# A different start and other load layouts for a linear-attention and ELU-MLP kernel on one core

## The chip, the cores and the metric

The kernel runs on one core of one Trainium2 chip. The metric is the device time of one execution in microseconds (us); lower is better. A core has a matrix engine (PE, whose weight loads are listed apart as PEld), a vector engine (DVE), a scalar engine (ACT) for exponentials and copies, GpSimd (POOL) and a sync engine (SP) that only issues transfers. Transfers (DMAs) are issued from queues of SP, ACT and POOL and carried by 16 DMA engines. POOL's own queue is the only one here that also changes the type (f32 to bf16) on the way.

## The reference

Inputs q, k, v are (8 batches, 8 heads, 576 positions, 64) in f32, w_phi is 64x128, w_in 512x2048, w_out 2048x512. The output is 4608x512 in f32.

```
def phi(x):
    proj = x @ w_phi
    proj = proj - max(abs(proj), axis=-1)
    return concatenate([exp(proj), exp(-proj)])
q_p, k_p = phi(q), phi(k)
kv  = sum over positions of k_p (outer) v
z   = sum over positions of k_p
out = (q_p @ kv) / (q_p . z + 1e-6)          # linear attention
x   = out, heads side by side: 4608 x 512
h   = x @ w_in
g   = h if h > 0 else exp(h) - 1             # ELU
return g @ w_out
```

## The kernel before, in words

**Attention.** The work is cut into 16 "quads": quad i is batch i//2 and four of its heads. In each head 512 positions are "main" and the last 64 are the "tail". For k and q, quad by quad: a transpose (kT, qT), a projection with w_phi (tile pk; for q also one with the operands exchanged, pq), the exponentials of plus and minus the projection on ACT (EK for keys at L697, Eq for queries at L851), and the row maximum of the magnitude on DVE (L659). The maxima of the keys give factors em on ACT (L726), and POOL multiplies v by them (vs at L748 for the main part, vst at L758 for the tail). PE then sums keys times values (pkv, L894), and queries times that (pn, L948 and L962). DVE combines the signs (tot, L997 and L1003), POOL divides (x, L1045 and L1074), and x is transposed (xT).

For the first five quads k and q are transposed on PE against an identity matrix (`ident`), L583 for the main part and L561 for the tails; later quads use transposing DMAs from SP. A tail transpose takes 64 positions of two heads, a 64x128 block. Tails of k and q of one batch share one staging tile t_b, k on partitions 0 to 63 and q on 64 to 127, loaded as 64 partitions of 8 heads with 64 numbers each.

**MLP.** Nine chunks of 512 tokens, one for each batch's main part and a ninth for all tails. mm1 (ph<-xT,w_in, L1241; for chunk 0 in halves of 256 tokens, L1256), exponential e on ACT (L1269), u = e − 1 on POOL (L1273), g = max(min(u, 0), h) on DVE (gT, L1285), mm2 (po<-w_out,gT, L1343), a copy out of PSUM to o_sb on ACT or DVE (L1369, three o_sb buffers), and a store (L1378, L1382). In mm1 the weights that are loaded into PE are 128 neighbouring columns of w_in, in mm2 they are 128 tokens of gT.

**What sets the order.** The order on each engine is written out while the program is built. A `Planner` (L125 to L315) is given every operation with an assumed cost per engine, what it depends on, and which of the eight PSUM banks it takes. It walks through assumed time and gives each engine that is free the ready operation of the lowest rank; where an operation may run on ACT or DVE, it chooses. The ranks are in the string RANKS, two characters for each operation in the order of their making. POOL may have up to eight loads outstanding. Before assumed time 60 the planner puts matrix products of zeros (`fill`, L1545) where it expects PE to idle, for half of the expected gap, and 32 of them stand at the start.

**The start.** SP's queue loads k half 0 of quad 0 (as f32, into buffers of v) and then w_phi twice (L1412, L1421), ACT's queue k half 1. ACT casts these to bf16 (L1443, L1454). POOL first builds the identity (L1427), and then issues casting loads, half of q, the k tails, half of k, k of batch 1, and then the rest of batches 0 and 1, w_in in two halves (L385) and w_out in four parts (L388), mixed by the planner with its arithmetic. w_in lies in one tile, with partition p holding row p of each block of 128; w_out likewise, so that each load of four blocks brings four separate rows of 512 numbers to each partition. Batches 2 and later are loaded when earlier quads have released the staging tiles (two buffers for each).

Of the kernel before, what the change touches and what calls it, by code (L numbers as in the profile page):

```python
# [34 lines left out]
    "00Fb02Fl011z8i04050309070B080A060D0F0H0K0C0M0J0G0d0e0ETUPETXPbE5OG2hOa9GN25g97E4"  # L35
    "Rt0W0TOm0R0SNX0b0QOC0P0OOk0Z0X0U0V320o0n0I0L0g0f6aLiLj0YKGKLKW6ZMdMf0N0cMM0a47Oc"
    "VTVQKKKFWECTOnAUNL45BmBiBs3C2F44BlBcBt3B2E432MB9Ba3637BY5T5V5F5O9i4L5qGp6DEI84IN"
    "E6Ml9HMs9FN38D8EKyWBVXK+MbMcMtMPMOKzMWWGNi2YMaWAMZ4M2t2Z2a2c3x3z38SnSlWCWHWDWF4B"
    "5859313A302-48MwWJVYWI4PWKAp2+Aa4g7F8M897I728J3E3S4Y3IFzFY9Y6+5S5v5J5KE33d3qEU6I"
    "5tAx6t2g6EDo4O6fCa2LFR9bC77R3XHu5w6T4q3rC95j6H6v5P7U6Y6eAJ5YH76w9w545p71AIAeCy6G"  # L40
    "4V9uAS3l7DBnAb3i4k7g7W5r9XLN7i5k7M5XDL7v7Z3L6N8B4f6p537z4d2b706L5sGTIk6l7o9rF69f"
    "AA6U85D1CmBH8oAdB0APD24l6O7p835yAE7G8N7x8O8g9T7r7w7s8w9pCx4R8FLa8e1V2zBS6W2U413-"
    "2O5D57BD4+50BE4v5ABF4y5I2N515B5G5H8P5d5f4n4o5m5l1wC0C18t8s8q8z1vCBCA9V9W8b8a567T"
    "3o3s8y9eA-65EA3M3W8h4h2P693O4m8l4i2R7YAH4x4T5R61628v8j91CFB3Kt8d1S2xCZ6X1W6x6y4Q"
    "CHCI4aCMCG4ZCQCO4XCPCdBA4p39CSCb3D6S66676F4j5N2w7L7K757476732X7a7b7Q7O7P7N6J7V3g"
    "3h775W3mAt2V5z8c685+8f6C6M4J5Q5x8Z6B5-6u40A8BhBg90A29DA99CCcGiCn929hAKFED0AQ7CEo"
    "9EA099EiTNFhEcGZW8JgDHILVrITB-FfUIIbE-FyVpW3FJI6BoW5BQHI8A869xEWAMDyCU2WAW6i2r6d"
    "AL6K9z2p9B987k796r9ZFc9cVqAX8HACGs3JFiFMGnI7Sp3KEpDuERF3ANC3BIDAGAGDFoE02v5M3u5U"
    "4C6hAzAw4rCjB2Ay4zCi3a7E818Y8U968R8S828T8X958Q8V64DnDm8WCDC8BwBuBxBvCgCf3N6c6bAD"
    "A5A4A63f8K8L8p8u8rCC2u6k7S78C655CoUOEFTPFdESTOF7EEW6GlGBV4HPGM4FGODVDK7B7ADS8x2e"  # L50
    "6P2j6V4D7JA79d9lAZ9gFrCRAB9+AR9m9n5nDDEG9v9tA39aGg9S9Q8IGd4WGyGvGXGUGVGQ4HCtCpEk"
    "EmEsEu8-BkC4C2Dx6zAOVBGI8n2k2q8m2Q2m603Z2s6q2i2oA+244sW1H3H4273FAFFZKXObEP8kAkSb"
    "He9-JDRhD9FIIyRIHpJQFmFpHcJSF9JAIDL2JF93I51oEHB1DlMI21LEIKA120LPIHFg88CeHGIMDbJb"
    "H08GCkBqJYEz9sKaDpEwECF5D7GjJlE8IOJhIwKx3+RBHkICGtIh9PTRGhHEEbD-BKDQDRD6DrDv5u4I"
    "4E7j6A7hCrDJAu4c7q7t7XWNWQWgWnWPWiWhWOWkWjWRWmWlFHWLWMWfWeW9WVWTWUWSWXWWAlWdWcCv"
    "ChCwCl5o4u4tWbWYWZWa7uFWCKCJDiAsENAmEVDW7eSgEQSi7d9jN87c8+QxQvDXTBT+RJF2FnUaUc87"
    "6-F1FX80AYBdAnBJBZAjAqBeAhAiBXAcAr9yBLBNBOBMIuEMELE1E2IrIsBVS6TyJMJRJPJLAgC+C-B6"
    "B7B8BBDYSsBzByJOHdTiD4SrIGBrB5IFB4LFDj9ULGDM949RIfATKZFDEqErR-RFDa6g4eHTF829DZHz"
    "DGIiHBISFBI4CqG8DkI8IjDPDB26JoBTHsFsEf8CI2LHIoFAGbHKJKExGoE7BCFjGmGkEKJwIaEDL0EJ"
    "GYBbI-G1GFBWFPKJGKAvK6GeFkG3FKFFIENeIQHWG+IRGHNRGuCYO8JBMxPOQaHmLOJfM1LbGRHjCsJ2"  # L60
    "KUBjD3BfV+DF3328DO6jCzBG9A1U1T9K1a1h9J1g1c9I1b1iQw1Q1R1Z1dG21p1m1l1n3435Dq1y1xId"
    "2I2J2KCW1+1-1r1q1u1sBUToJNL3IcF4G6D86RDCEj5iHnBP4-HoBR52DwHy9qDE635h7fI0H-O7ItB+"
    "C53bD+AGDN4w3w3p6s3t3k6m3n3j6o3y3vJH3P3T2C2B5Z5c7-5e5a7y7+D55C5E49424A46CV3Y3V4U"
    "4K4N4SEBKY3e3c3QIlEOIA3UFwG0KIH5HLH9FqEaJUFuEYEZH6GcHAGzEdEeJTJ7MjJEFLJ6InIzI9M8"
    "MkK5GwJXJ9KOGLHOLkKHH8FGK-HgIJHMKiJzIeF+LmGxU7HNN-DzDUIqL1NtEnOrLWIBFNLMGCKcEtN5"
    "MePyJnHFQyK4IpKjNUQuE9LINWS9JZO3MEMgPMP9QEK1O5Q-QmUo7HPaRQTJMBMUVsNIM9IvMJQ3ReK2"
    "1k221j234G6QGfDh3R4bFt1GE+1814Ev1617F0191DEy151A5L1H1I1C1BFCDfDeDcDgEgEhGaFUFV1M"
    "1L1N1OGGGPGS1X1f1Y1eGWI11F1E2yNHDsNGDtM5JWKpKVHQF-M4M7G4MFMAHHJ-K7HJO2JIJJKEJ+5b"
    "TaG9FQFxFvP0Q4QBP2QfQ6P7QCQ7P5QDQFMn9k9oQdQJGqOAOEOFODGrDdGJRKRMT2T5T3T7HiNPNQUU"
    "UDUSUBNYO1PnPpP1JcH+ImKAOTT1SzK0N4PsOSS+S-JyRYTMNvP+TQSj3G3HPYO4RbVJR9TFPz2HN1U3"  # L70
    "QH2TLBPKR02fNMPqQ+2lLtOwQpAVTAPCQRCERcPGQVRpHlOYQZPBSUOLQgM0QcRERyTdPiOPS5VWPPVa"
    "SxVMMiLAR1ViRgLXPZV8PXU9LzTgMXUNQbS3L+LeUiSALVO6LqLpCXR6LsL-LDLfTZTDM-MzRURSJpLl"
    "GE1JDI1KG5EXPmKmJkJ3HDMhKBHvHqJ5LKHrK9HxIxK8I+LLHUHSHRLSLQJeDTElG-FOKPJmJxNAN99N"
    "9M9L9OJiPuPt7lCN7m7nNTLJPRPQ1tNwTVIgTSIYVEUKIZVKUEIUVCUFIVVuUHIWVvURRfSBSCMVMHK3"
    "JCETPoIXJjPT0q0wPS0l0sPV0t0mPW0p0uJ413Kb0v0r110x0y0+0z0-10L8RzUQ0j0h0i0kKDVtVoRl"
    "RkRsRqL9Ri1P122GLgNBLhMuQUPNOZQ9OHPHQ8OBPFQYP6OdRdPIPLROPhPjJdNZLYUjUqVANaCuUWTp"
    "LwUMUTTfLoUYSMVmMDVfSVUCLcV3VGN6KeVgW7VRR+V-V9MoSZS0VDOMKhTYUePARXSwVZNSSaS4UZOW"
    "SuOgUwORRVRvVeS2SWR4RAMySYQMSPMqTCLuLvLxQGTHJqHCI3KrQjNxQoKQKRKqRTQSKoJtJuKkMmQ5"
    "G7J0J1BpQIOiHtJvKuOOLTONTnUnUmTmUbUhTtUpUfT-UvU+SXAoAfUyUsQQShSdRHRGSfQXL7UVUX2S"
    "2D2n2ALUVPVSFSFeFTFaPxPwCL2dU5KMVwKNVxM+NfNgRRNhTxKCV1U1KwV0TvKvU2TwNyVHVIM6LrR7"  # L80
    "LdKsNrLnJaVkHZHwVlU4HXVOHaHVVjHYHbVnRnRoVdVcU-SLSJV6SKV7V2KSNcNdVUVNVhVVLRUJUGUt"
    "TlUuTkQrRDTbTcU0L4T9KfRPSvVLMrKgOXNORWOVNKL5OUN+L6S1LZMvT8T6TITGJrQWUdPcJsUgSeLC"
    "KlTWMKRLJVU8UPPrJGQAGNQqKnVFQeSTNkMCR5OpM3KdRjSDNzOIP-OqNbSNKTQ2NDNVQLUzNqSGJ8Rr"
    "NsRaQOQzNETjQiMGMSQlOeTqNmSOR8QKM2NpNlOjNoO0OoMLPeOtSmQsMpP3O+MRVzNJOvPkOyUkOlPJ"
    "NnQhNuRCO-VbRZU6OxSqT4RuMQMYPUS7OsV5UrSoMNOKQtTuPdQPQ0TTPfTzTsNCNFR2QnTeO9MTT0Rm"
    "PgOQP8UxOzUASyPvOuTrLyQkP4OfSSRNPDUlSETEPlSRS8SQH2HfIIIPSHStN7NNOJOhULTLVyW0W2W4"
    "QTTKRwRxQ1ScSFSIQNSkN0Nj6nH1Th25HhR3"
# [231 lines left out]
def kernel(  # L319
# [11 lines left out]
    P = 128  # L331
# [46 lines left out]
    w_in_sb = consts.tile([P, N_CT, DFF], BF16)  # L378
    w_in_r = moe_w_in.rearrange("(ct p) j -> p ct j", p=P)
    w_out_sb = consts.tile([P, N_JT, DM], BF16)  # L380
    w_out_r = moe_w_out.rearrange("(jt p) o -> p jt o", p=P)

    def load_w_in(half):
        j = slice(half * (DFF // 2), (half + 1) * (DFF // 2))
        nc.gpsimd.dma_start(out=w_in_sb[:, :, j], in_=w_in_r[:, :, j])  # L385

    def load_w_out(jt):
        nc.gpsimd.dma_start(  # L388
            out=w_out_sb[:, jt:jt + 4, :], in_=w_out_r[:, jt:jt + 4, :]
        )  # L390
# [10 lines left out]
    def staged(b, n):  # L401
        if (b, n) not in kqv:
            kqv[b, n] = stage.tile(
                [P, H * D if n == 3 else BW],
                FP32 if n == 2 else BF16,
                name="kqvt"[n] + "_b",
            )
        return kqv[b, n]
# [9 lines left out]
    def load_tails(eng, n, b):  # L418
        if n < 2:
            eng.dma_start(  # L420
                out=staged(b, 3)[n * TAIL:(n + 1) * TAIL, :].rearrange(
                    "p (h d) -> p h d", d=D
                ),
                in_=(k, q)[n][b, :, MAIN:S, :].rearrange("h j d -> j h d"),
            )
            return
# [66 lines left out]
    def plan_quad(i):  # L493
# [33 lines left out]
        for n in range(2):  # L527
# [30 lines left out]
            def tail_transpose(e, n=n, t0=t0, tr_rows=tr_rows, trt=trt):  # L558
                t = psum(trt, [P, P], BF16, "trt")
                for s in range(2):  # L560
                    nc.tensor.transpose(  # L561
                        t[:, s * TAIL:(s + 1) * TAIL],
                        kqv[b, 3][tr_rows, t0 + s * P:t0 + (s + 1) * P],
                        ident[tr_rows, tr_rows],
                    )

            def tail_copy(e, n=n, trt=trt):
                f = nc.scalar.copy if e == "ACT" else nc.vector.tensor_copy
                f(in_tile(n)[:, 8, :], trt.tile)
# [7 lines left out]
            for j0, j1 in parts:  # L577
# [10 lines left out]
                def copy(e, tr=tr, j0=j0, j1=j1, n=n):  # L588
# [6 lines left out]
                    [main if len(parts) < 2 else landed[0, 0, 3 + j0 // 4], *prior],  # L595
# [14 lines left out]
            o2 = add({"PE": 0.06}, tail_transpose, [tail], new=[trt], key=key + 0.01)  # L610
# [158 lines left out]
        for c in range(3):  # L769
            for sg in range(2):  # L770
                vs_ops[c].append(
                    add(
                        {"POOL": 1.0 if c < 2 else 0.58},
# [14 lines left out]
        for c in range(3):  # L788
# [3 lines left out]
            def queries(e, c=c, pair=pair, pair_f=pair_f):  # L792
                blocks = slice(c, 8, 2) if halves else slice(4 * c, 4 * c + 4)
                project_halves(1, range(8)[blocks], pair)
                for par in range(2):
# [10 lines left out]
            def tail_queries(e, pair=pair, pair_f=pair_f):  # L806
# [11 lines left out]
            o = add(  # L818
                {"PE": 0.44 if c < 2 else 0.22},
                queries if c < 2 else tail_queries,  # L820
                [moved[1][0 if c < 2 else 1], *old("out")],
                new=pair + pair_f,
                mode=1 if c < 2 else 0,
                key=first + 0.4 + 0.2 * c,
            )
            ops["q"].append(o)
# [12 lines left out]
            for par, bank in enumerate(pair_f):  # L839
# [13 lines left out]
                for sg in range(2):  # L853
# [4 lines left out]
                            [o, landed["zero"]] if c == 2 else [o],  # L858
# [27 lines left out]
        for s in range(2):  # L886
# [24 lines left out]
            def kv_copy(e, s=s, bank=bank):  # L911
# [6 lines left out]
                {"PE": 0.65},  # L918
# [501 lines left out]
    for c in range(2):  # L1420
        nc.sync.dma_start(out=wst[c * D:(c + 1) * D, :], in_=w_phi)  # L1421
# [160 lines left out]
```

## Time and profile before

| | |
|---|---|
| median of 3 runs | 360.99 us (360.65 to 361.04) |
| the profiled execution | 361.48 us |
| its span, first to last instruction | 359.6 us |
| PE busy | 346.3 us (96%), of it fills from 0 to 50 us: 13.98 |
| DVE, ACT, POOL busy | 268.8, 256.5, 244.7 us |
| granted PE clock | 1.00 throughout |
| DMA | 86668 packets, 43.46 MB |
| first exponential of keys (EK, ACT) | starts at 7.36 us |
| first scaling of v (vs, POOL) | starts at 14.56 us |
| first product of mm1 / of mm2 | starts at 33.9 / 42.3 us |

Times inside a profile are counted from the start of the span. A busy PE is not PE at its peak, since the ends of pipelined products are modelled. A number in brackets behind an instruction is the idle time of its engine just before it, with what ended it.

### The profile page before, as it was taken

The numbers are of one execution on the slowest core, as the hardware profiler recorded it, in microseconds if no ns is written. First come the engines' busy times: TensorE is split into PE (matmuls) and PEld (weight loads), VectorE is DVE, ScalarE is ACT, GpSimd is POOL, SyncE is SP. The second block draws the span as 40 slices with busy tenths as digits, with TensorE's granted clock in tenths as the row PEclk, the third lists the DMA queues.
The fourth block names the chain that finished last, engine by engine and source line by source line (L and its number), as shares of the span: only waits on it lengthen the run. The fifth ranks groups of instructions, "written<-read, shape, count | busy, mean of one in ns | idle before, by whom it ended". The sixth has DMA issues, their size and how long they took to land.

```text
span 359.6 us, 8973 instructions
## 1 busy us (share of the span) xinstructions
PE 346.3 (96%) x3379; PEld 196.5 (55%) x3427; DVE 268.8 (75%) x580; ACT 256.5 (71%) x565; POOL 244.7 (68%) x342
## 2 busy tenths in 40 slices
PE   8888999999999999999999999999999999999995
PEld 7666776656554655455545555554456444444444
DVE  5989878989998899769977989999866812662600
ACT  5999977799779777985599888596994514553521
POOL 8699999298969797697677697366379622552500
PEclk9999999999999999999999999999999999999999
DMA  9999999999699799599759606682210331001013
GB/s 145 285 221 206 204 188 119 217 131 141 91 186 212 110 203 126 143 113 234 77 133 187 98 6 129 121 170 58 56 40 30 66 91 60 0 29 41 20 58 89
DMA packets 86668, 43.46 MB, mean 121 GB/s; under 512 B 55648, under 2 KB 80608, under 8 KB 86624
## 3 DMA queue, kind: packets, MB, share of 16 engines
q1 hardware_dynamic: 57632, 26.62, 36.5%
q0 software_dynamic: 28320, 15.47, 33.2%
q10 hardware_dynamic: 672, 0.79, 0.8%
q8 instruction: 27, 0.44, 0.5%
q14 instruction: 17, 0.14, 0.1%
HBM read 36.77 MB, written 9.44 MB: 128 GB/s over the span
## 4 chain that ended last, share of the span: by engine, by line
PE 78%; POOL 7%; ACT 4%; DVE 4%; DMA 3%; issue 3%; SPq 0%; POOLq 0%; ACTq 0%
PE po L1343 33%; PE ph L1241 27%; PE pk L638 4%; PE pkv L894 4%; PE pn L948 3%; POOL vs L748 2%; DVE gT L1285 2%; ACT EK L697 2%; PE ph L1256 2%; DMA qT<-t_b 2%; PE pq L798 2%; DMA e_sb<-in_w_phi_dram 1%; POOL u_sb L1273 1%; ACT Eq L851 1%; POOL vst L758 1%
## 5 line engine op out<-in xcount | busy, mean ns | idle before, releaser
L1343 PE MATMUL po<-w_out_sb,gT 128*128 128x512 bf16 (+1 forms) x562 | 131.9, 373 | 1.7 <-issue 0.3
L1273 POOL TENSOR_SCALAR u_sb<-e_sb 128x512 bf16<-128x512 f32 x144 | 88.3, 620 | 64.8 <-ACT e_sb L1269 54.6
L1285 DVE SCALAR_TENSOR_TENSOR gT<-u_sb,ph 128x512 bf16<-128x512 bf16 x144 | 95.8, 680 | 41.6 <-POOL u_sb L1273 41.4
L1269 ACT ACTIVATE e_sb<-ph 128x512 f32<-128x512 f32 x144 | 86.8, 620 | 46.6 <-PE ph L1241 37.4
L1241 PE MATMUL ph<-xT,w_in_sb 128*128 128x512 bf16 x430 | 105.2, 379 | 1.1
L1343 PEld LDWEIGHTS <-gT 128*128 128x128 bf16 x592 | 54.2, 98 | 58.9 <-issue 3.6
L851 ACT ACTIVATE Eq<-pq 128x512 bf16<-128x512 f32 x128 | 68.9, 618 | 10.0 <-PE pq L798 9.7
L1241 PEld LDWEIGHTS <-w_in_sb 128*128 128x128 bf16 x512 | 47.3, 98 | 51.0 <-issue 1.4
L697 ACT ACTIVATE EK<-pk 128x512 bf16<-128x512 f32 x128 | 69.1, 649 | 5.6 <-PE pk L638 5.4
L748 POOL TENSOR_TENSOR vs<-v_b,em 128x512 bf16<-128x512 f32 x64 | 65.5, 1045 | 1.0 <-DMA v_b<-in_v_dram 0.9
L659 DVE TENSOR_REDUCE m_q<-pk 128x4 f32<-128x512 f32 (+1 forms) x80 | 47.7, 628 | 6.3 <-PE pk L638 5.7
L659 DVE TENSOR_REDUCE m_k<-pk 128x4 f32<-128x512 f32 (+1 forms) x80 | 47.5, 629 | 6.3 <-PE pk L638 5.4
L1045 POOL TENSOR_TENSOR x<-tot,rec 128x576 bf16<-128x576 f32 x28 | 31.7, 1154 | 17.6 <-DVE rec L1041 10.6
L1369 ACT COPY o_sb<-po 128x512 f32<-128x512 f32 (+1 forms) x22 | 12.6, 572 | 28.9 <-PE po L1343 28.9
L997 DVE TENSOR_TENSOR tot<-pn,w 128x260 f32<-128x260 f32 x64 | 26.1, 422 | 5.0 <-POOL x L1045 2.2
L1003 DVE TENSOR_TENSOR tot<-tot,pn 128x260 f32<-128x260 f32 x64 | 25.7, 418 | 0.4
L948 PEld LDWEIGHTS <-Eq 128*128 128x128 bf16 x448 | 19.7, 97 | 9.5 <-issue 0.8
L758 POOL TENSOR_TENSOR vst<-v_tail,em 128x260 bf16<-128x260 f32 x32 | 19.5, 623 | 4.0 <-ACT em L726 3.9
L948 PE MATMUL pn<-kv,Eq 128*128 128x65 bf16 x448 | 21.6, 194 | 0.4
L894 PEld LDWEIGHTS <-EK 128*128 128x128 bf16 x512 | 18.8, 98 | 4.5 <-issue 0.4
L894 PE MATMUL pkv<-vs,EK 128*128 128x65 bf16 x512 | 20.9, 194 | 0.1
L1256 PE MATMUL ph<-xT,w_in_sb 128*128 128x256 bf16 x128 | 17.5, 273 | 0.2
(89 smaller groups left out, 322.1 us busy)
## 6 DMA issues: line engine op xcount, KB each, us to landing
out_dram<-o_sb SPq DMA_DIRECT2D x32, 256.0 KB, 2.3
v_b<-in_v_dram SPq DMA_DIRECT2D x6, 1024.0 KB, 6.8
k_b<-in_k_dram POOLq DMA_DIRECT2D x7, 512.0 KB, 8.7
q_b<-in_q_dram POOLq DMA_DIRECT2D x7, 512.0 KB, 10.7
w_out_sb<-in_moe_w_out_dram POOLq DMA_DIRECT2D x4, 512.0 KB, 18.3
w_in_sb<-in_moe_w_in_dram POOLq DMA_DIRECT2D x2, 1024.0 KB, 19.7
v_b<-in_v_dram POOLq DMA_DIRECT2D x2, 512.0 KB, 10.5
v_b<-in_v_dram POOLq DMA_DIRECT2D x1, 1024.0 KB, 13.2
```

Of the source, the lines that this page charges most:

```text
L659: nc.vector.tensor_reduce(dst, src, axis=AX.X, op=ALU.max, apply_absolute_value=True)
L697: nc.scalar.activation(EK()[:, 2 * c + par, sg, :] if c < 2 else EKt[:, sg, :], bank.tile[:, 0:n, :].rearrange("p a b -> p (a b)"), ACT.Ex ...
L748: nc.gpsimd.tensor_tensor(st["vs"][:, sg, :, r, 0:D], kqv[b, 2][:, o:o + 2 * HW].rearrange("p (c n d) -> p c n d", c=2, d=D), by_head(st[" ...
L851: nc.scalar.activation(dst, src, ACT.Exp, scale=1.0 - 2.0 * sg)
L894: nc.tensor.matmul(pkv[:, c, sg, :], st["EK"][:, 2 * s + t % 2, sg, (2 * c + t // 2) * F:(2 * c + t // 2 + 1) * F,] if t < NT else EKt[:, ...
L948: nc.tensor.matmul(pt[:, t, :], st["Eq"][:, par, s, sg, o:o + P], st["kv"][:, s, c, sg, :], start=True, stop=True,)
L1045: (nc.vector if e == "DVE" else nc.gpsimd).tensor_tensor(tile("x", work, [P, NS, 2, D], BF16)[:, :, c, :], tot[:, r, 0:D], st["rec"][:, r, ...
L1241: nc.tensor.matmul(ph, w_in_sb[:, ct, jt * P:(jt + 1) * P], xTs[ch][:, ct, :] if ch < B else xT_tail[:, ct // 2, :, ct % 2, :], start=(ct ...
L1269: nc.scalar.activation(t["e"], flat(bank.tile), ACT.Exp)
L1273: nc.gpsimd.tensor_scalar(t["u"], t["e"], -1.0, 1.0, op0=ALU.add, op1=ALU.mult)
L1285: nc.vector.scalar_tensor_tensor(dst, u, 0.0, bank.tile, op0=ALU.min, op1=ALU.max)
L1343: nc.tensor.matmul(bank.tile, gTs[ch][:, jt, tt * P:(tt + 1) * P], w_out_sb[:, jt, o0:o1], start=(jt == 0), stop=(jt == N_JT - 1),)
```

## The change

- **Identity.** It is no longer built first: it becomes an operation of the planner, on POOL behind the first three loads, and the transposes on PE depend on it. POOL's first loads are now, in this order, the k tails of batch 0, half of k, half of v.
- **First loads of the other queues.** ACT's queue takes k half 0 and then one half of w_phi; SP's queue takes the other half of w_phi and then k half 1. The cast of w_phi may run on ACT or DVE.
- **w_out.** Row 4p + j of each group of 512 goes to partition p, slot j, so four rows that are neighbours in memory lie side by side in a partition: 4 KB in bf16 at once instead of four times 1 KB.
- **w_in.** Two tiles instead of one, one for each half. As the rows of w_out are now dealt to partitions in steps of four, the columns of w_in have to be too: the weights of one product are 128 columns with a step of 4.
- **Tails of batches 0 and 1.** Two neighbouring positions go to one partition: 32 partitions of 8 heads with 128 numbers. Each tail is then transposed by eight products of 32x64 blocks instead of two of 64x128, and the copy out of PSUM puts the positions in order. The staging tile is twice as wide. Later batches stay as they are.
- **Query projections.** For batches 0 and 1 the two kinds (pk and pq) are two operations that take two PSUM banks each; for later batches one operation with four, as before for all.
- **o_sb** has two buffers instead of three.
- **Costs and ranks.** Assumed costs and sizes of some operations are set anew (shown below), and RANKS is another string, so the order of the work changes on every engine.

```diff
 RANKS = (
...
-    w_in_sb = consts.tile([P, N_CT, DFF], BF16)
+    w_in_halves = [
+        consts.tile([P, N_CT, DFF // 2], BF16, name=f"w_in{j}") for j in range(2)
+    ]
-    w_out_r = moe_w_out.rearrange("(jt p) o -> p jt o", p=P)
+    w_out_r = moe_w_out.rearrange("(g p j) o -> p g j o", p=P, j=4)
...
+    def w_in_of(ct, jt):
+        half, jt = divmod(jt, N_JT // 2)
+        j = jt // 4 * CHUNK + jt % 4
+        return w_in_halves[half][:, ct, j:j + CHUNK - 3:4]
...
     def load_w_out(jt):
         nc.gpsimd.dma_start(
-            out=w_out_sb[:, jt:jt + 4, :], in_=w_out_r[:, jt:jt + 4, :]
+            out=w_out_sb[:, jt:jt + 4, :], in_=w_out_r[:, jt // 4]
         )
...
     def load_tails(eng, n, b):
+        if n < 2 and b < 2:
+            eng.dma_start(
+                out=staged(b, 3)[n * 32:(n + 1) * 32, :].rearrange(
+                    "p (h x) -> p h x", h=H
+                ),
+                in_=(k, q)[n][b, :, MAIN:S, :].rearrange(
+                    "h (p t) d -> p h (t d)", t=2
+                ),
+            )
+            return
...
             def tail_transpose(e, n=n, t0=t0, tr_rows=tr_rows, trt=trt):
...
+                r = slice(n * 32, (n + 1) * 32)
                 for s in range(2):
...
+                    for c in range(2):
+                        for par in range(2):
+                            o = 2 * t0 + (4 * s + 2 * c + par) * D
+                            nc.tensor.transpose(
+                                t[c * D:(c + 1) * D, s * TAIL + par * 32:][:, 0:32],
+                                kqv[b, 3][r, o:o + D],
+                                ident[r, r],
+                            )
...
-            def queries(e, c=c, pair=pair, pair_f=pair_f):
+            def queries(e, pair=pair, blocks=blocks):
                 project_halves(1, range(8)[blocks], pair)
+
+            def queries_f(e, pair_f=pair_f, blocks=blocks):
...
+            elif c < 2:
+                o = add({"PE": 0.22}, queries, deps, new=pair, mode=1, key=key)
+                o_f = add({"PE": 0.22}, queries_f, deps, new=pair_f, mode=1, key=key)
...
-                t["o"] = moesm.tile([P, DM], FP32, name="o_sb", bufs=3)[:, o0:o1]
+                t["o"] = moesm.tile([P, DM], FP32, name="o_sb", bufs=2)[:, o0:o1]
...
-    for c, eng in enumerate((nc.sync, nc.scalar)):
+    for c, eng in enumerate((nc.scalar, nc.sync)):
+        w = wst[c * D:(c + 1) * D, :]
+        if c:
+            eng.dma_start(out=w, in_=w_phi)
         eng.dma_start(
...
-    for c in range(2):
-        nc.sync.dma_start(out=wst[c * D:(c + 1) * D, :], in_=w_phi)
+        if not c:
+            eng.dma_start(out=w, in_=w_phi)
...
-    make_identity(nc, ident)
...
+    start = add({"DVE": 2.4}, lambda e: None, key=-9.0)
+    landed["ident"] = add({"POOL": 0.45}, lambda e: make_identity(nc, ident), key=-5.5)
...
-    landed["zero"] = add({"DVE": 1.15}, clear, key=-9.0)
+    landed["zero"] = add({"DVE": 1.15}, clear, [start], key=-9.0)
...
-            load((b, n, 1), 0.24, 0.7, lambda e: load_tails(nc.gpsimd, n, b))
+            load((b, n, 1), 0.15, 0.7, lambda e: load_tails(nc.gpsimd, n, b))
...
-        load(("w_out", part), 0.95, 0.77, lambda e, part=part: load_w_out(4 * part))
+        load(("w_out", part), 0.8, 0.77, lambda e, part=part: load_w_out(4 * part))
```

## The prediction

> **What bounds the kernel now.** I read the page's busy table first, then its releasers, then the trace cut into stretches of time, and last the chain of waits and the timeline of the start.
>
> The busy table of the page:
>
> ```profile
> span 359.6 us, 8973 instructions
> PE 346.3 (96%) x3379; PEld 196.5 (55%) x3427; DVE 268.8 (75%) x580; ACT 256.5 (71%) x565; POOL 244.7 (68%) x342
> ```
>
> PE is idle for 13.3 us only. Busy time per stretch (columns: stretch, length, PE, weight loads, DVE, ACT, POOL, clock, DMA share, GB/s) shows where:
>
> ```profile
> 0.00:10.00 10.00, 8.00 (x89) 6.74 (x89) 6.16 (x20) 5.75 (x12) 8.61 (x16) 1.00 0.97 150
> 10.00:20.00 10.00, 8.72 (x130) 6.58 (x131) 9.43 (x20) 9.98 (x28) 7.19 (x10) 1.00 1.26 289
> 20.00:30.00 10.00, 7.77 (x167) 6.33 (x163) 8.87 (x25) 9.71 (x29) 9.99 (x14) 1.00 1.19 208
> 30.00:40.00 10.00, 9.08 (x149) 7.60 (x146) 8.99 (x26) 9.79 (x24) 9.93 (x16) 1.00 1.30 204
> 40.00:50.00 10.00, 9.84 (x124) 7.12 (x124) 7.80 (x19) 8.92 (x21) 9.96 (x17) 1.00 1.37 201
> 340.00:359.60 19.60, 15.95 (x89) 8.60 (x88) 1.37 (x2) 3.69 (x7) 0.71 (x2) 1.00 0.24 68
> ```
>
> 6.4 of the 13.3 idle us lie before 40 us, 3.65 after 340 us, 3.2 between. PE's early busy time is partly false: the same view for the fill tile alone (products of zeros that nobody reads) gives 6.00, 3.97, 2.62, 0.88 and 0.51 us in the first five rows. So PE lacks real work for 6.4 + 13.5 = 20 us before 40 us, is full from there to 340 us, and then drains. What fills the first 40 us is POOL and ACT. The chain of waits names them in turn:
>
> ```profile
> 1.88 4.70 DMA e_sb<-in_w_phi_dram
> 7.36 4.06 ACT EK L697 x8
> 22.98 1.56 POOL w_out_sb L388 x2
> 26.04 3.89 POOL vs L748 x4
> ```
>
> The timeline of the start (start, length, engine, instruction, idle before and releaser):
>
> ```profile
> 0.74 0.20 POOL masks.py:197 MEMSET ident<- 128x128 bf16 x1 [0.29 <-POOLq L1566]
> 1.45 0.98 POOL L411 DMA_DIRECT2D q_b<-in_q_dram  x1
> 6.60 0.29 ACT L1454 CAST w_phi_both<-e_sb 64x128 bf16<-64x128 f32 x1 [1.23 <-DMA e_sb<-in_w_phi_dram]
> 10.16 0.77 POOL L388 DMA_DIRECT2D w_out_sb<-in_moe_w_out_dram  x1 [0.44 <-DMA k_b<-in_k_dram]
> 12.88 0.74 POOL L385 DMA_DIRECT2D w_in_sb<-in_moe_w_in_dram  x1 [0.72 <-DMA k_b<-in_k_dram]
> 14.56 1.05 POOL L748 TENSOR_TENSOR vs<-v_b,em 128x512 bf16<-128x512 f32 x1 [0.94 <-DMA v_b<-in_v_dram]
> ```
>
> From 14.56 us to 60 us POOL never rests (9.99, 9.93, 9.96, 9.93 of 10). Its first v scaling waits for a v load that was fourth of the large ones in a full DMA queue; two issues wait for earlier loads to land. ACT begins its exponentials at 7.36, behind a w_phi half that needed 4.7 us.
>
> **What the Trainium skill says.** DMA: Bandwidth & Descriptors, "Issuing engines are not separate DMA queues", says that all issuers feed the same DMA engines. The trace agrees: the first w_phi half took about 2.6 us from issue, the second 4.7, because POOL's packets had begun at 3.96. The same page, "Why small descriptors are slow", says each piece has a fixed cost; here a 128-byte packet takes 31 ns, 512 bytes 60, 1 KB 97, 2 KB 173. TensorE: Matmul & The Clock Gate, "Weight-path perf modes", allows fast weight loading for 128 columns, packed or strided, so a column step of 4 should load as fast; before has only packed weights (98 ns a record). SBUF — State Buffer, "Door 1: The DMA port swizzle", bears on the tails, now on 32 partitions instead of 64; no run here shows it.
>
> **The change, part by part.**
>
> *Identity behind the first three loads, tails first.* Before, POOL's first issue starts at 1.45, behind about 0.7 us of identity; its first packet moves at 3.96, 1.53 after that issue ends. After, the k tails are issued at about 0.74 (0.70 long), packets at about 3.0, landing at 4.4 to 4.9. The loads behind gain about 0.7, and the order puts half of k and half of v second and third, so v lands at about 8.3 rather than 14.48. The first v scaling is then released by ACT's em, not by v: 10.6 us of POOL work stand before it now, 9.8 after, and about 1 to 2 us of waits are left of 4. Start about 10.9 to 11.7, 2.9 to 3.6 earlier.
>
> *First hardware-queue loads.* ACT's queue takes k half 0 and a w_phi half, SP's a w_phi half and k half 1. Each w_phi half is now first or second, ahead of POOL's packets: cast at about 4.8 instead of 6.60. EK can start at 6.2 to 6.5 instead of 7.36, provided the tail transposes, now first in PE's queue, do not hold up the k transposes. About −0.9 for ACT and DVE.
>
> *Packets.* Four w_out loads: 512 pieces of 1 KB become 128 of 4 KB. 512 × 97 ns over 16 engines are 3.1 us; 128 at twice the 173 ns of a 2 KB piece 2.8: 0.3 each, 1.2 in all. Four tails: 512 × 31 ns/16 = 1.0 us become 256 of about 40 (between the rows for 128 and 512 bytes), 0.65: 0.3 each, 1.2. With the earlier start, the last w_out would land at about 42 instead of 45.4. This moves nothing that PE waits for by itself; the cover is POOL's own lateness. w_in in two tiles removes nothing by itself: the halves are loaded separately already.
>
> *Tail transposes.* 64 of 64x32 for 16 of 128x64: 64 × 30 ns (65-column pairs run at 29) minus 16 × 30, about +1.4 us of PE, before 40 us. If PE is short of work there it is free; I charge it in full, since PE work in order sets how much is left at 40 us.
>
> *Queries split, two output buffers, new ranks.* The split lets q projections start with 2 free banks instead of 4; the instruction count is the same. The ranks move work: up to the first mm1 group POOL has 29.9 us before and 30.5 after, ACT 27.3 and 26.8, PE 12.9 and 14.3; up to the eighth elu 53.2 and 50.6, 43.1 and 43.2, 31.8 and 31.6 (counts in program order by the mean durations of their groups). ACT takes seven kv copies and four output copies more, DVE fewer; both have 25% of slack over the span. Output buffers at two: an output store lands 2.3 us after issue, mm2 groups come 4 us or more apart (16 × 216 ns with mm1 between), so nothing.
>
> *Sum.* At the eighth elu (56.0 us), time minus PE's work in order is 24.3 us before: that is PE's whole lateness. POOL's is 4.0 to 4.4 from 14.56 on. After: POOL is 3 us earlier at its first scaling; ACT and EK allow only 0.9 of this at once, but ACT too loses 1.5 of lateness between 7 and 38 us to waits for the same late loads. I take PE's lateness at 40 us down by 3.1 to 21.2, and PE's work up by 1.4: net −1.7. As a check, the written-out program has 93 fills after the first 32 for 107: 14 × 56 ns of fill, each standing for twice that in planned gap, 1.57 us. From 40 us on PE is the bound in both, and the last stretch (3.65) stays. Span 359.6 − 1.7 = 357.9; the profiled execution 361.48 − 1.7 = 359.8. That execution is 0.5 above the median of the runs, 360.99; so the median is forecast at **359.3 us**.
>
> *Unknown costs.* Strided weights: 640 loads; at the skill's word 0, at worst each one slower than its matmul can hide. The nearest row is 98 ns against 216 (512 columns: hidden even at double) and 109 (256 columns: 128 loads of up to 90 ns more, 11 us if doubled). I take 0; the upper end is 3 to 5[...]. Tails in 32 partitions: between −0.3 and +0.3 each. The first POOL issue as opener: 0.70 to 0.98.
>
> **Rivals.**
>
> *A. Hidden (within 0.2%).* The front gain of POOL is spent elsewhere: ACT is 97 to 100% busy from 10 to 40 us with nearly the same work, so only 0.9 (EK) can be gained, and the 1.4 us of transposes fall on PE. Net between −0.5 and +0.5: 360.5 to 361.5. For it: ACT's rows. Against: idle notes show ACT late by waits, not by work alone.
>
> *B. Slower: the tails stall PE at its head.* PE's first real work is sixteen small transposes of k tails of quads 0 and 1, waiting for POOL's first load and identity; k transposes queue behind. From landing to EK stand 0.5 of small transposes, 0.3 of k's, a copy of 0.42 and a projection of 0.2, so it decides from a landing at about 5.9 us. At 7.5 EK begins at 8.9: +1.5 for every engine and +1.4 of PE's work, less 1.5 kept by the better load order: 362.4. For it: the first POOL packet moved 1.53 us after its issue ended and the tail load before took from 2.44 to 8.01. Against: there it queued behind 256 KB of q.
>
> *C. Slower by strided weights:* 256-column groups exposed, +2 to +5 over A: 363 to 365. For: no trace has such weights. Against: the skill's range.
>
> *D. More:* POOL keeps all of its 3 us and ACT follows: PE's lateness −4.2 for 1.4 of work, −2.8: 358.2.
>
> *E. The change doesn't do what it says:* PE drains late because the new order leaves a larger last mm2 run (100 matmuls after the last mm1 instead of 84). These cost PE the same, but the last store has less ahead: within ±0.4.
>
> **How the numbers follow.** No difference can be told within 0.2%, 0.72 us, of 360.99. My forecast (358.3 to 360.2) has 0.45; D 0.20; A 0.15 (some on each side of the bound); B 0.12; C 0.05; E 0.03. Faster: 0.45 + 0.20 + a few of A = 0.68. Same: most of A, E and a strip of the forecast, 0.14. Slower: B, C, 0.18. The range of 8 in 10 leaves out C, the far half of B and the far end of D: 357.5 to 361.9. The likeliest case alone: 358.3 to 360.2.
>
> **What would show it.** Right: EK begins at 6.2 to 6.6; the first v scaling at 11 to 12 us, released by ACT; fills under 13 us; PE's idle before 40 us together with fills down from 20 by about 3; mean of mm1 weight loads still 98 ns; the span from 100 us on the same shape, shifted by about 1.7. Wrong: EK at 7.4 or later with PE waiting for t_b (B); mm1 rows with long idle "issue" or loads far above 98 ns (C); vs early but the first mm1 group no earlier (A); new idle of PE late in the span, waiting for an output copy (two buffers).

## The result, and the profile after

| | before | after |
|---|---|---|
| median of 20 runs each | 361.47 us (360.44 to 364.43) | 360.55 us (358.78 to 361.46) |
| ratio | | 0.9949, interval 0.9928 to 0.9969 |
| the profiled execution | 361.48 us | 360.78 us |
| its span | 359.6 us | 359.0 us |

The change makes the kernel 0.5% faster by the ratio, which compares runs made beside each other (1.8 us, interval 1.1 to 2.6); the medians of all runs lie 0.9 us apart and the profiled executions 0.7. The time and the gain are close to the forecast. The way there is not: the start became slower, the new layouts and the edits to the first loads show no effect, and the order of the work without them gives nearly the whole gain.

The busy table of the kernel after:

```profile
span 359.0 us, 9073 instructions
PE 350.1 (98%) x3461; PEld 206.8 (58%) x3461; DVE 265.2 (74%) x568; ACT 260.0 (72%) x577; POOL 242.9 (68%) x342
```

Busy time by stretch, columns as before (stretch, length, PE, weight loads, DVE, ACT, POOL, clock, DMA share, GB/s):

```profile
0.00:10.00 10.00, 6.87 (x87) 5.89 (x88) 4.78 (x15) 4.79 (x9) 8.12 (x17) 0.91 0.93 179
10.00:20.00 10.00, 8.95 (x128) 6.87 (x126) 9.40 (x20) 9.88 (x26) 7.65 (x10) 0.84 1.29 225
20.00:30.00 10.00, 9.96 (x188) 8.07 (x187) 8.62 (x25) 9.31 (x29) 8.53 (x13) 0.91 1.20 255
30.00:40.00 10.00, 8.90 (x157) 7.08 (x153) 9.44 (x29) 8.63 (x21) 9.93 (x16) 1.00 1.12 213
340.00:359.00 19.00, 15.39 (x88) 8.33 (x85) 0.00 (x0) 3.09 (x6) 0.00 (x0) 1.00 0.27 75
```

The reader is to see three things. In the first row every engine was busy for less than before (PE 6.87 against 8.00, DVE 4.78 against 6.16, ACT 4.79 against 5.75, POOL 8.12 against 8.61): the start is later. The clock is 0.91, 0.84 and 0.91 in the first three rows, where it was 1.00 before. And a busy PE is no good measure here: fills are in it (5.23, 4.78, 2.75 and 0.88 us in the first four rows), and a product at half the clock counts twice its time. The trace of before also lacks 48 of its 3427 products, so the 3.2 us of idle PE that the prediction counted between 40 and 340 us are largely gaps in the records; 48 products at 216 ns would be 10 us. From here on I therefore go by when the same piece of work starts, and where busy time is used I say what it hides.

The chain of waits (start, length, what), its beginning and end:

```profile
1.33 5.28 DMA t_b<-in_k_dram
13.01 2.89 DVE m_k L702 x5
...
337.22 18.18 PE po L1399 x100
```

The chain starts with the load of the k tails. The timeline (start, length, engine, instruction, idle before and releaser) shows why:

```profile
1.33 0.78 POOL L427 DMA_DIRECT2D t_b<-in_k_dram  x1 [0.88 <-POOLq L1625]
3.78 0.62 ACT L1503 CAST k_b<-v_b 128x512 bf16<-128x512 f32 x1 [0.42 <-DMA v_b<-in_k_dram]
6.65 0.43 PE L590 MATMUL trt<-ident,t_b 32*64 32x32 bf16 x16 [2.06 <-DMA t_b<-in_k_dram]
8.41 2.79 ACT L740 ACTIVATE EK<-pk 128x512 bf16<-128x512 f32 x5 [1.34 <-PE pk L681]
```

k half 0 is cast by 4.4 us, but PE waits until 6.6 for tails that it needs only later, since their transposes stand first in its queue. The first EK starts 1.05 us later than before. The first v scaling starts at 13.41 instead of 14.56, no longer waiting for v, as forecast in kind but 2 us later than forecast.

### The profile page after: what moved, and what is told of

The parts are those of the page before. It is cut to its first block, busy times and chain, and to the rows that moved or that the text cites. A ratio compares the mean times of both kernels' runs of the same rounds, so it can differ in the third digit from the quotient of the medians.

```text
span 359.0 us, 9073 instructions
## 1 busy us (share of the span) xinstructions
PE 350.1 (98%) x3461; PEld 206.8 (58%) x3461; DVE 265.2 (74%) x568; ACT 260.0 (72%) x577; POOL 242.9 (68%) x342
## 4 chain that ended last, share of the span: by engine, by line
PE 93%; DVE 3%; DMA 1%; ACT 1%; issue 0%; POOLq 0%
PE po L1399 35%; PE ph L1297 31%; PE pk L681 5%; PE pkv L950 5%; PE ph L1312 4%; PE pn L1004 4%; PE pq L844 2%; DVE m_k L702 2%; DMA t_b<-in_k_dram 1%; PE tr L616 1%; PE fill L1604 1%; PE pnt L1032 1%; PE pk L663 1%; DVE tot L1053 0%; ACT Eq L907 0%; PE pq L856 0%
## 5 line engine op out<-in xcount | busy, mean ns | idle before, releaser
L1399 PE MATMUL po<-w_out_sb,gT 128*128 128x512 bf16 (+1 forms) x592 | 135.5, 374 | 0.0
L1341 DVE SCALAR_TENSOR_TENSOR gT<-u_sb,ph 128x512 bf16<-128x512 bf16 x144 | 96.8, 682 | 40.0 <-POOL u_sb L1329 39.4
L1297 PE MATMUL ph<-xT,w_in 128*128 128x512 bf16 x448 | 106.8, 380 | 0.0
L1297 PEld LDWEIGHTS <-w_in 128*128 128x128 bf16 x512 | 54.9, 114 | 45.2 <-issue 1.6
L1425 ACT COPY o_sb<-po 128x512 f32<-128x512 f32 (+1 forms) x26 | 14.9, 573 | 34.2 <-PE po L1399 34.0
L1312 PE MATMUL ph<-xT,w_in 128*128 128x256 bf16 x128 | 17.9, 275 | 0.2
```

The lines of the kernel that those rows point to most:

```text
L1297: nc.tensor.matmul(ph, w_in_of(ct, jt), xTs[ch][:, ct, :] if ch < B else xT_tail[:, ct // 2, :, ct % 2, :], start=(ct == 0), stop=(ct == N ...
L1312: nc.tensor.matmul(bank.tile[:, j, :], w_in_of(ct, jt + j), xTs[ch][:, ct, hf * CHUNK // 2:(hf + 1) * CHUNK // 2], start=(j == 0 and ct == 0),
L1341: nc.vector.scalar_tensor_tensor(dst, u, 0.0, bank.tile, op0=ALU.min, op1=ALU.max)
L1399: nc.tensor.matmul(bank.tile, gTs[ch][:, jt, tt * P:(tt + 1) * P], w_out_sb[:, jt, o0:o1], start=(jt == 0), stop=(jt == N_JT - 1),)
```

## The experiments

Two theories stood against each other. **Loads:** the new layouts and the edits to the start (identity, first loads of SP and ACT) give the gain. **Order:** the new ranks give it without them. The order in which POOL issues its loads comes from the ranks too, so in these experiments it belongs to the order. The planner's costs and ranks were left alone in each kernel, so that it keeps the order of the kernel that it is made from on every engine, except for the edit itself. Ratios are to the kernel before in the same series, so two kernels of different series are compared by way of the kernel before; differences of 0.002 between rows are within the intervals.

| kernel | ratio | interval |
|---|---|---|
| after | 0.9949 | 0.9928 to 0.9969 |
| after, identity first | 0.9954 | 0.9936 to 0.9971 |
| after, old weight layouts | 0.9950 | 0.9931 to 0.9968 |
| after, old tails | 0.9972 | 0.9955 to 0.9988 |
| after, old first loads | 0.9945 | 0.9927 to 0.9963 |
| new order alone, all four undone | 0.9958 | 0.9938 to 0.9977 |
| old order with the load and start edits, two output buffers | 1.0068 | 1.0040 to 1.0096 |
| before with two output buffers | 1.0050 | 1.0028 to 1.0072 |
| old order with loads, old tails, three buffers | 0.9997 | 0.9973 to 1.0021 |
| after, tails' transposes later | 0.9940 | 0.9914 to 0.9967 |
| the same with both k halves first | 0.9950 | 0.9932 to 0.9968 |
| the same with identity first | 0.9914 | 0.9885 to 0.9943 |
| after, 76 fills at the start | 0.9979 | 0.9963 to 0.9996 |

**Undoing one part at a time.** Identity first:

```diff
+    make_identity(nc, ident)
...
-    landed["ident"] = add({"POOL": 0.45}, lambda e: make_identity(nc, ident), key=-5.5)
+    landed["ident"] = add({"POOL": 0.45}, lambda e: None, key=-5.5)
```

> The kernel after with one thing undone: the identity is built ahead of POOL's first issue, all else in the same order. Theory 1 (a delay at the start reaches the end, because PE waits for the k tails and every engine starts behind it): the first issue moves from 1.33 to about 1.6 or later, the tails land at about 7.0 to 7.3 instead of 6.6, the first EK starts at 8.8 to 9.1 instead of 8.41, and the time is 0.3 to 0.7 us longer than that of the kernel after. Theory 2 (the start is absorbed, the gain comes from the order in the later stages): first EK later by the same amount, the time within 0.2 us of the kernel after.

The ratio is that of the kernel after. The first EK was even earlier in this profile, at 7.65, as PE waited 1.4 us for the tails instead of 2.06. From the issue of the first POOL load to PE's first use of it passed 4.4 us here, 5.3 in the kernel after, and 4.7 in the next kernel, whose start is that of the kernel after: this time differs by more from one profile to the next than the identity can shift it. The first issue starts at 1.5 instead of 1.33: the identity delays it by 0.2 us, where I had counted 0.7.

The old layouts of w_out and w_in:

```diff
-        j = jt // 4 * CHUNK + jt % 4
-        return w_in_halves[half][:, ct, j:j + CHUNK - 3:4]
+        return w_in_halves[half][:, ct, jt * P:(jt + 1) * P]
...
-    w_out_r = moe_w_out.rearrange("(g p j) o -> p g j o", p=P, j=4)
+    w_out_r = moe_w_out.rearrange("(g j p) o -> p g j o", p=P, j=4)
```

> The kernel after with the old layout of w_out and w_in: 1 KB pieces and weights of 128 neighbouring columns, same order. If the larger packets carry the gain: the last w_out load lands about 1.2 us later and the time rises by 0.5 to 0.9 us. If they are hidden: within 0.2 us. If weights with a column step of 4 cost time (rival C): the mm1 weight loads go from 114 ns back to 98 and the time falls by 0.5 us or more.

The ratio does not move: neither the larger packets nor the columns in steps of 4 show an effect. The intervals reach 0.2% to each side, and since both were undone at once, a gain of one and a loss of the other below that could hide each other. The groups of instructions (line, operation, count, busy time and mean ns, idle) of the kernel after show that the weight loads themselves are slower:

```profile
L1297 PEld LDWEIGHTS <-w_in 128*128 128x128 bf16 x512 | 54.9, 114 | 45.2 <-issue 1.6
```

and with the old layout they are back where they were:

```profile
L1296 PEld LDWEIGHTS <-w_in 128*128 128x128 bf16 x512 | 47.4, 98 | 51.7 <-issue 1.6
```

The 16 ns lie beside a product of 216 ns: over consecutive w_in products, loads start 180 ns apart on average in the kernel before and in the kernel after alike (some 555 pairs each, 256-column products among them). By this pitch the strided weights cost nothing, and rival C fell.

The old tails:

```diff
-        if n < 2 and b < 2:
+        if n < 2 and b < 0:      # so too where the tails are transposed and copied
```

> The kernel after with the old layout of the k and q tails of batches 0 and 1 (512 pieces of 128 bytes for a load, two transposes of 64x128 for a tail instead of eight of 32x64), same order. By my sum PE has 0.9 to 1.4 us less work and each tail load takes about 0.3 us longer: the time falls by 0.5 to 1.4 us if PE's work counts in full, rises by about 0.3 if the first load, for which PE waits, decides, and stays within 0.2 if both are hidden or cancel.

0.9972 against 0.9949 with overlapping intervals: if anything the old tails are slower, and the 1.4 us that I charged PE for the small transposes do not come out. They run in a part where PE is filled with zeros. The profile of this kernel bears on the clock, below: PE waits here almost as long as in the kernel after (2.06 us),

```profile
6.50 0.39 PE L579 MATMUL trt<-ident,t_b 64*128 64x64 bf16 x4 [1.91 <-DMA t_b<-in_k_dram]
```

yet its granted clock is 1.00 throughout the first 40 us.

The old first loads of SP and ACT:

```diff
-    for c, eng in enumerate((nc.scalar, nc.sync)):
+    for c, eng in enumerate((nc.sync, nc.scalar)):
...
+    for c in range(2):
+        nc.sync.dma_start(out=wst[c * D:(c + 1) * D, :], in_=w_phi)
```

> The kernel after with the first loads of SP and ACT as before (SP: k half 0, w_phi twice; ACT: k half 1), same order. PE's wait for the k tails stands ahead of everything in both, so if that wait hides the first loads: within 0.2 us of the kernel after. If the second w_phi half, now behind POOL's packets, lands at 6.5 or later: its cast ends at about 7.2 and k half 1 is cast behind it at 7.8, EK starts about 0.2 us later and the second group of projections about 0.7 us later: 0.2 to 0.7 us longer.

No difference, 0.9945: in its profile PE waited for the tails (1.2 us) in this kernel too, and the first loads can hide behind that.

**Order alone, and loads alone.** With all four undone at once, by the diffs above, only the order (that of POOL's loads included: k tails, half of k, half of v still come first), the split queries, the two output buffers and the second tile of w_in remain:

```diff
+    make_identity(nc, ident)
...
+        return w_in_halves[half][:, ct, jt * P:(jt + 1) * P]
...
+        if n < 2 and b < 0:
...
+    for c, eng in enumerate((nc.sync, nc.scalar)):
```

> The kernel after with all of its load and start edits undone (identity first, old layout of w_out and w_in, old tails, old first loads of SP and ACT) and only the new order, the split queries and the two output buffers left. If the order carries the gain: the ratio to the kernel before is within 0.2% of that of the kernel after (0.9949), the span about 359 us. If the loads carry it: 0.998 to 1.002.

0.9958, practically the whole gain; the profiled span was 358.1 us. Its stretches:

```profile
0.00:10.00 10.00, 7.67 (x80) 6.54 (x81) 4.88 (x17) 4.89 (x9) 8.84 (x17) 1.00 0.93 174
10.00:20.00 10.00, 8.16 (x123) 6.04 (x121) 9.25 (x20) 9.98 (x26) 7.46 (x10) 1.00 1.34 224
20.00:30.00 10.00, 9.58 (x200) 7.51 (x197) 9.35 (x26) 9.92 (x31) 9.98 (x15) 1.00 1.22 251
30.00:40.00 10.00, 8.90 (x125) 6.39 (x122) 8.82 (x30) 8.73 (x21) 9.97 (x16) 1.00 1.24 208
```

PE's busy time less fills (5.58, 4.12, 2.30, 0.88) is 21.4 us here; before it was 33.57 − 13.47 = 20.1. That looks like 1.3 us more work in the first 40 us, but busy time misleads here too. Counted by the trace, 389 real products start before 40 us, against 392 before: eight of 128 columns and two of 256 fewer, four of 512 and a few small ones more. At pitches of 0.216 us for 512 columns, 0.109 for 256 and 0.055 for 128 that is only some 0.3 us more. The first mm1 product even comes later than the 33.9 of before, and the eighth elu earlier. The order alone, and below it the kernel before:

```profile
34.47 0.60 PE L1311 MATMUL ph<-xT,w_in 128*128 128x256 bf16 x4
...
53.91 1.28 DVE L1340 SCALAR_TENSOR_TENSOR gT<-u_sb,ph 128x512 bf16<-128x512 bf16 x2
```

```profile
56.04 0.69 DVE L1285 SCALAR_TENSOR_TENSOR gT<-u_sb,ph 128x512 bf16<-128x512 bf16 x1
```

Here less PE work stands ahead of the eighth elu, so this alone is no gain. I estimate where the gain arises by giving each weight load of the two traces the pitch of its product: time less PE's work is then lower than before by 0.3 us at 40 us, by 0.7 at 100 and by 1.5 to 1.7 at 200 and 300. Most of the gain thus comes after the start, where PE has no fills.

What this kernel does not separate are the parts that are left in it: the ranks, the order of POOL's loads, and the split queries.

The reverse is the old order with the new layouts, first loads and identity. The wider tail tiles leave no memory for a third output buffer, so it has two:

```diff
-    w_out_r = moe_w_out.rearrange("(jt p) o -> p jt o", p=P)
+    w_out_r = moe_w_out.rearrange("(g p j) o -> p g j o", p=P, j=4)
...       # w_in in halves with step 4, tails, first loads as in the kernel after
+            if len(issued) == 3:
+                make_identity(nc, ident)
...
-                t["o"] = moesm.tile([P, DM], FP32, name="o_sb", bufs=3)[:, o0:o1]
+                t["o"] = moesm.tile([P, DM], FP32, name="o_sb", bufs=2)[:, o0:o1]
```

> The kernel before, in its own order, with the load and start edits (w_out in 4 KB pieces, w_in in two tiles with step 4, tails of batches 0 and 1 on 32 partitions, first loads of SP and ACT as in the kernel after with the cast of w_phi ahead of that of k half 1, the identity behind POOL's first three issues, two output buffers). If the loads carry the gain: 0.994 to 0.997. If the order carries it: 0.998 to 1.002, with PE's extra 0.9 us of small transposes in it.

It is slower by 0.7%, beyond both expectations. Among the waits of DVE was one of 3.0 us that neither before nor after has, for an output store. So I tried that buffer alone, in the kernel before:

```diff
-                t["o"] = moesm.tile([P, DM], FP32, name="o_sb", bufs=3)[:, o0:o1]
+                t["o"] = moesm.tile([P, DM], FP32, name="o_sb", bufs=2)[:, o0:o1]
```

> The kernel before with two output buffers instead of three and nothing else. In the run with the load and start edits in the old order a copy to o_sb on DVE waited 3.0 us for an output store, at about 113 to 116 us. If the missing third buffer is what made that kernel slower: the same wait shows here, and the ratio to the kernel before is 1.004 to 1.008. If it was the loads: 0.999 to 1.001.

1.0050: the buffer was most of it. The timeline of this kernel:

```profile
113.63 3.79 SPq L1378 DMA_DIRECT2D out_dram<-o_sb  x3
...
116.37 0.69 DVE L1369 COPY o_sb<-po 128x512 f32<-128x512 f32 x1 [2.67 <-DMA out_dram<-o_sb]
...
117.11 0.39 PE L798 MATMUL pq<-qT,w_phi_both 64*128 64x512 bf16 x2 [0.94 <-DVE o_sb L1369]
```

A store stood late in SP's queue (the chain of waits has SP's transposes, 1.86 and 1.23 us, just ahead of it), the copy on DVE waited for it 2.67 us, and PE for the copy. In the kernel after nothing waits for an output store. So two buffers, which cost 0.5% in the old order, show no such wait in the new one.

With three buffers and the old tails, the remaining load and start edits could be tried fairly in the old order:

```diff
-    w_out_r = moe_w_out.rearrange("(jt p) o -> p jt o", p=P)
+    w_out_r = moe_w_out.rearrange("(g p j) o -> p g j o", p=P, j=4)
...       # w_in in halves with step 4, first loads as in the kernel after
-    make_identity(nc, ident)
...
+            if len(issued) == 3:
+                make_identity(nc, ident)
```

> The kernel before, in its own order and with its three output buffers and old tails, with the other load and start edits (w_out in 4 KB pieces, w_in with step 4, new first loads of SP and ACT, identity behind POOL's first three issues). If the loads are worth something in the old order: 0.996 to 0.999, with the first scaling of v at about 13.4 instead of 14.56 us. If they are hidden: 0.999 to 1.001.

0.9997: no gain that can be seen, though the interval, 0.9973 to 1.0021, would still hold half of that of the kernel after. Its timeline shows the earlier scaling arriving and vanishing (the profiled execution, 365.07 us, was the longest of its 14, but what made it long came after these lines):

```profile
13.12 1.05 POOL L761 TENSOR_TENSOR vs<-v_b,em 128x512 bf16<-128x512 f32 x1
...
38.21 0.71 ACT L1282 ACTIVATE e_sb<-ph 128x512 f32<-128x512 f32 x1
```

The second of these in the kernel before:

```profile
38.29 0.65 ACT L1269 ACTIVATE e_sb<-ph 128x512 f32<-128x512 f32 x1
```

Scaling begins 1.44 us earlier than the 14.56 of before, but the exponential of the first mm1 group starts at 38.21 for 38.29. POOL's 1.4 us are gone 25 us later, with ACT at 10.00, 9.70 and 9.95 of 10 us between 10 and 40 us. That is rival A's mechanism. ACT itself began no earlier: k half 1 was cast at 6.14 only, and the first EK came at 7.72, 0.36 later than before. The first scaling with the order alone, at 13.18 us, is hardly later than the 13.12 here, so an early first scaling does not make the gain by itself.

**The wait for the tails.** The sixteen transposes moved behind the second group of key projections:

```diff
+                if i < 2 and n == 0 and not late:
+                    deferred.append(lambda f=tail_transpose_of[i]: f[0](e, late=True))
+                    return
...
+                if i == 0 and cs == (1,):
+                    for f in deferred:
+                        f()
```

> The kernel after with the sixteen transposes of the k tails of quads 0 and 1 moved on PE from the head to behind the second group of key projections of quad 0. PE then doesn't wait 2.06 us for the tails ahead of the k transposes. Theory 1: the first EK starts at 5.6 to 6.5 instead of 8.41, PE's clock stays at 1.00 over the first 20 us, and the time falls by 0.6 to 1.6 us. Theory 2: the first EK is as early, but POOL and the loads don't follow, and the time is within 0.3 us.

The timeline and stretches of this kernel:

```profile
6.73 0.40 PE L623 MATMUL tr<-ident,k_b 128*128 128x128 bf16 x4 [1.13 <-ACT k_b L1513]
7.53 2.56 ACT L750 ACTIVATE EK<-pk 128x512 bf16<-128x512 f32 x5 [0.85 <-PE pk L688]
```

```profile
8.00:12.00 4.00, 3.51 (x76) 3.08 (x73) 3.96 (x10) 4.00 (x13) 2.24 (x4) 1.00 1.35 222
18.00:22.00 4.00, 3.98 (x71) 2.71 (x69) 3.42 (x8) 4.00 (x13) 3.59 (x8) 1.00 1.13 229
```

In the kernel after the same two stretches read:

```profile
8.00:12.00 4.00, 4.00 (x46) 3.36 (x47) 3.16 (x7) 3.46 (x8) 2.21 (x3) 0.57 1.36 240
18.00:22.00 4.00, 4.00 (x50) 3.03 (x50) 2.54 (x7) 4.00 (x10) 4.00 (x8) 0.57 1.12 242
```

The wait for the tails is gone, and the next one, for k half 1 behind w_phi on SP, is 1.13 us, so EK is 0.9 us earlier and not 2 to 3. This profiled execution had a span of 357.0, 2.0 below that of the kernel after. The timed ratio is only 0.9940: that is 0.0009 below the kernel after, about 0.3 us, which the intervals do not separate.

Two attempts at k half 1. Both k halves ahead of w_phi on their queues, on top of the last edit:

```diff
-        if c:
-            eng.dma_start(out=w, in_=w_phi)
         eng.dma_start(
...
-        if not c:
-            eng.dma_start(out=w, in_=w_phi)
+        eng.dma_start(out=w, in_=w_phi)
```

> The kernel after with the k tails' transposes moved behind the first key projections, as in the run before, and on SP k half 1 ahead of the w_phi half, as on ACT. If what is left of the start's delay is k half 1 (it was cast at 6.06 to 6.68, and PE waited 1.1 us for it): it is cast by 5.8, the first EK starts at 6.3 to 6.8 instead of 7.53, and the profiled span is 0.7 to 1.2 us below that with the tails moved alone (357.0). If w_phi now comes late (landing above 5.5): no gain, within 0.3 us.

No gain (0.9950): k half 0 was now cast at 4.85 instead of 3.89, k half 1 at 6.08, behind w_phi on ACT, and EK began at 7.97. Instead of this, the tails later and the identity first, by the same two lines as in the first experiment, so that POOL's packets begin later:

```diff
+    make_identity(nc, ident)
...
-    landed["ident"] = add({"POOL": 0.45}, lambda e: make_identity(nc, ident), key=-5.5)
+    landed["ident"] = add({"POOL": 0.45}, lambda e: None, key=-5.5)
```

> The kernel after with the k tails' transposes behind the first key projections and the identity built first: POOL's packets begin about 0.7 us later and leave k half 1 more room. If k half 1 is what holds the start now: cast at about 5.4 instead of 6.06, the first EK at 6.9 to 7.2 instead of 7.53, the time 0.3 to 0.6 us below that with the tails moved alone (ratio about 0.993). If POOL's later loads count as much: within 0.2 us of it.

k half 1 was cast at 6.09 and EK began at 7.56, neither as expected. Yet 0.9914 (0.9885 to 0.9943) is the lowest ratio of all, a median of 359.15 us of 8 runs. It beats the kernel before; against the kernel after the intervals still overlap by 0.0015, so that it is better is likely and not shown. Its cause isn't either.

**The clock.** PE idles for 2 us at the start of the kernel after, and a few us later its clock is half for 3.4 us, twice (0.57 over the 4 us shown above). To keep PE busy:

```diff
-    fill(7, 32)
+    fill(7, 76)
```

> The kernel after with 76 products of zeros at the start instead of 32, so that PE stays busy until about 6 us, while it waits for the k tails. If the wait of 2.06 us is what lowers PE's clock to about half in two stretches of 4 us between 8 and 22 us: the clock stays at 1.00 in the first 30 us. If that lower clock costs time: 0.3 to 0.8 us less than the kernel after; if PE has room there, within 0.2 us.

In the profile the clock stays at 1.00:

```profile
8.00:12.00 4.00, 3.35 (x66) 2.67 (x60) 3.38 (x8) 2.50 (x6) 2.21 (x3) 1.00 1.39 238
18.00:22.00 4.00, 3.90 (x59) 2.55 (x57) 3.64 (x9) 4.00 (x10) 4.00 (x7) 1.00 1.14 232
```

But the fills ran until 7.8 us, not 6, so the first EK began at 9.50, 1.09 later than in the kernel after, and the first mm1 exponential at 39.87, in both. In these two profiles, then, a start 1.09 us later at full clock gives the same as the earlier one at the lower clock; the span was 359.0 twice. Timed, the kernel comes out slower than the kernel after (0.9979; intervals overlap slightly), and it was the wrong cure: the fills stand in front of work that could have begun. Nor did they keep the clock up: of its 22 timed executions 13 had a mean clock below 0.9965, six of them 0.989, as low as in the profile with two such stretches.

That the idle 2 us cause the low clock is not shown, and the length of the wait does not decide it. The profiles with identity first and the tails later (1.65 us of waiting), with identity first (1.4) and with the old weights (1.5) had both stretches, and the one with the old first loads (1.2) one of them; those with the tails alone moved (1.13) and with the order alone (1.33) had none, but nor had the old tails, at 1.91.

## Why the prediction was right or wrong

The time, 360.55, lies in the range (357.5 to 361.9) but above that of the likeliest case (358.3 to 360.2), as the medians lie 0.9 us apart only; the forecast gain of 1.7 us lies in the interval of the ratio. Most of its terms were wrong all the same, so that the number was met by luck: the start that was to bring the gain got worse, and an order that had been given no gain of its own made up for it. Of the signs named for a right forecast most failed: EK at 8.41, the first scaling at 13.41, fills of 13.6 us before 40 us, fills and PE's idle time together down by 0.9 instead of 3, weight loads of mm1 at 114 ns. Step by step:

- *What bounds the kernel.* Right that the first 40 us are where PE lacks work and ACT and POOL set the pace. The idle of 3.2 us in the middle was mostly missing records, a misreading without effect on the sum.
- *Identity behind the loads, tails first.* Wrong in its size and in what it would do. The issue starts at 1.33 and not at 0.74, because POOL idles 0.88 us before it anyway, identity or not. The load takes 5.28 us from there; I had added 1.5 us of start-up and a guess for packets, and landed at 4.4 to 4.9. It lands at 6.6. The first v scaling came at 13.4, not 11: it was released by em, as forecast, but em stands on ACT behind EKs that began 1 us later, not 1 us earlier.
- *First hardware-queue loads.* k half 0 was cast from 3.8 us and w_phi by 4.9, as forecast; k half 1, which I had not followed, only at 6.45. Undone, nothing changes.
- *Packets.* "This moves nothing that PE waits for by itself" held: 0.9950 without them, 0.9997 with them in the old order.
- *Tail transposes.* +1.4 us of PE charged in full; without them the kernel was not faster (0.9972). It was a term of the sum that should have been about 0: in the filled stretch PE's work can replace fills, and I had named that case before charging it.
- *Two output buffers.* "Nothing" was right for the new order and wrong as reasoned: mm2 groups 4 us apart do not protect a copy whose store is stuck behind transposes in SP's queue. In the old order it costs 0.5%.
- *The sum.* The step that failed is "POOL is 3 us earlier at its first scaling" and, from it, PE's lateness at 40 us "down by 3.1". The first scaling came 1.15 us earlier, at the eighth elu PE's lateness in order fell by 1.0 (24.3 to 23.3), and the edits that I gave as its cause show no gain alone (0.9997). In place of it stands the order: 0.9958 without those edits, with only about 0.3 us of it by 40 us and the rest later, where I had forecast none. The check by the number of fills, 1.57 us, came close in number, but it too speaks of the start.
- *Strided weights.* Taken at 0, as the skill's word allowed (TensorE: Matmul & The Clock Gate, "Weight-path perf modes"); the pitch agrees (180 ns in both), though the record of a load grows from 98 to 114 ns.
- *Rival B* is what the start does: the landing at 6.6 lies past the 5.9 from which it decides, and EK is 1.05 later for 1.5 forecast. It did not make the kernel slower, since the order gains more. *Rival A* is what the new loads do in the old order.

What in the order does it is only read, not tested. Between the 8th and the last elu the kernel with the order alone takes 283.8 us and the kernel before 286.7, with 2.3 us less of PE work placed there by the pitches above, so about 0.6 us is left. In that part PE goes 32 times from a long product with 128-row weights to 64-row weights, against 35 before. By the trace such a step mostly starts 0.52 us behind the last weight load instead of 0.216, 0.3 us lost, so three fewer would be worth about 0.9 us. Here is one of the kernel before:

```profile
71.06 0.10 PEld L1343 LDWEIGHTS <-gT 128*128 128x128 bf16 x1
...
71.58 0.45 PEld L638 LDWEIGHTS <-kT 64*128 64x128 bf16 x16 [0.42 <-issue]
```

The two sizes are alike, no more; other steps differ between the orders too, and no run changed that number alone.

## What to carry to other kernels

When a change brings a new order and new transfers together, run each alone before believing either: here every edit to a layout or to the first loads had a good reason and showed no effect, and the new order did the work. A resource such as a buffer count belongs to the order it was chosen for, and taking it over into another order can cost more than the change gains. Ask what stands behind the first instruction of an in-order queue when it waits for a load whose result is needed late: with the tails' transposes moved EK began 0.9 us earlier, though the gain in time, about 0.3 us, was too small to be told here.

## What was not expected of the hardware

- PE's granted clock drops to half for 3.4 us (0.57 over 4 us) a few us after the first wait of PE, and again ten us later; it appears in some executions and not in others of the same kernel. In one series 6 of 48 timed executions of the kernel before had a mean clock below 0.9965; of the kernel after it were 14 of 20. The Trainium skill (TensorE: Matmul & The Clock Gate, "HAM oscillation — how this bites in real kernels") speaks of gaps over about 3.4 us; here the longest wait ahead of it was 2.06 us, and 1.91 us went without it.
- Its price can be estimated. In the four profiles with both stretches 26.5 us pass from the first v scaling to the first mm1 exponential, in the other six of kernels with the new order 25.5 to 25.8, so 0.7 to 1.0 us are lost there. Over the 152 timed executions of these ten kernels, the 25 with a mean clock of 0.991 or less were 0.55 us longer (standard error 0.15) than those at 0.998 or more of the same kernel.
- The first casting load of POOL, 64 KB, lands 5.28 us after its issue starts in the kernel after; in two other profiles PE used it 4.4 and 4.7 us after that.
- A weight load with a column step of 4 takes 114 ns instead of 98 by its record, with no change of the pitch (180 ns on average in both).
